# Output products of a unit one gap later, column-norm loads one step ahead, whole-row sums in the last pair

## The chip, the cores and the metric

The kernel runs on one core of one Trainium2 chip. The metric is the device time of one execution in microseconds (us), the median of several runs; lower is better. Engines are named as in the profile: PE is TensorE (PEld its weight loads), ACT is ScalarE, DVE is VectorE, POOL is GpSimd, SP is SyncE. POOL and SP issue the transfers (DMAs) that this text speaks of.

## The reference

Channel attention, then a feed-forward layer with SiLU and no gate of its own:

```python
qn = q / (norm(q, axis=1) + 1e-06); kn = k / (norm(k, axis=1) + 1e-06)   # q, k, v: 2 x 6016 x 256
s  = kn.transpose(0, 2, 1) @ qn / tau                                   # 2 x 256 x 256
a  = softmax(s)
x  = (v @ a).reshape(12032, 256)
h  = x @ w_in                                                           # 256 -> 2048
out = (h / (1 + exp(-h))) @ w_out                                       # 2048 -> 256
```

## The kernel before, in words

The output is made in twelve pairs (`pairs`): for each of the two batches b, five of 1024 tokens and one of 896. The attention matrix is folded into `w_in` (`mix`), so a pair needs two large products, v times the mixed weights and the SiLU of that times `w_out`. Each f32 operand is split into a high and a low f16 part and three products of the parts are made; both products use a seven-product (Strassen-Winograd) scheme, so sums and differences of blocks are operands too.

Pairs 0 and 5 go through `emit_pair_group`. The other ten (`paired`) go through `emit_unit`: eight units u each, U0 to U7 below, four of which (`q` from 0 to 3) add into one set of four PSUM banks, named a, b, c and d. A unit has four gaps; each begins with input products (`product`, six matmuls each: three in gap 0, two in gap 1, one each in gaps 2 and 3), and then the main loop pops output products from the list `ready`, up to a cost of 8, 12, 16 and 8, where each entry costs 4 and is four matmuls: 2, 3, 4 and 2 entries, 11 in all. The input products go through the three banks y, x and z, which ACT copies and DVE subtracts (`minus`), then ACT applies SiLU (`silu`), rounds the result to the high f16 part (`high`), and DVE makes the low part (`rest`). The upper two blocks of a unit are b11 and b12 (`tops`), the lower two b21 and b22 (`lows`).

`out_of_unit` queues what follows a unit. Its output products are lists: `now` (seven entries, from b11 to b22 themselves), `then` (from the sums t1, t2, t3) and one from t4 that goes behind the next unit's. The sums and the products are not emitted at once. `later(n, ...)` hangs a call on the n-th gap from here, and `tail` runs what hangs on the current gap. t1 (= b11 + b12) and, but for the last unit of four, t4 (= t2 + b21) are made by pairs of DMAs on POOL's queue, a copy and then one that adds (`accum_op`) and therefore waits for the copy to land; t2 and t3 are DVE's (`plus`). At the fourth unit of each set, ACT takes the four banks out (`take`), DVE joins them (`join`), and `leave` adds and stores.

In the ten paired pairs the order of instructions on PE, DVE and ACT is the order of the program text (`manual_schedule`), and each engine works through its own list strictly in that order. POOL and SP also execute their own lists in order.

Beside the units run steps of other work, spread by the main loop behind the gaps: `scale_v` (the next pair's v: maximum, scale, splits; three steps a unit), the loads of the next v, and, in pairs 1 to 3, `square_sums`: 24 steps, one a unit in gap 1, that each load a stretch of the transposed q or k of the second batch (tile `turned`) and have ACT sum its squares. `turned` and the tile of t2 and t3 (`t23`) rotate through the same seven buffers (`st`).

Of the kernel before, what the change touches and what calls it, by code (L numbers as in the profile page):

```python
# [9 lines left out]
F32 = mybir.dt.float32  # L10
# [4 lines left out]
AF = mybir.ActivationFunctionType  # L15
ALU = mybir.AluOpType
AX = mybir.AxisListType
PSUM = bass.MemoryType.PSUM
P = 128
# [11 lines left out]
def channel_attention_then_silu_ffn(ctx, tc, kq, qT, kT, vT, tau, w_in, w_out, outT):  # L31
    nc = tc.nc
    B, N, _, C = kq.shape
    DFF = w_in.shape[1]
    KC = C // P
# [4 lines left out]
    NT = 1024  # L40
# [40 lines left out]
    def room(name, n=1):  # L81

        k = turns[name] + turns[name] % n
        size = rooms[name].shape[1]
        k %= size
        turns[name] = (k + n) % size
        return rooms[name][:, k] if n == 1 else rooms[name][:, k : k + n]
# [158 lines left out]
    def square_sums():  # L246

        edges = list(range(0, N, NT)) + [N]
        m = sm.tile([P, 2 * KC, len(edges) - 1], F32, tag="squares", name="squares", bufs=1)
        norms[0] = m  # L250
        yield
        for i, x in enumerate((qT, kT)):
            for cb in range(KC):
                for g, (u, w) in enumerate(zip(edges, edges[1:])):
                    t = st.tile([P, NT], F32, tag="st", name="turned", bufs=7)
                    nc.sync.dma_start(t[:, : w - u], x[cb * P : (cb + 1) * P, u:w])
                    sq = st.tile([P, NT], F32, tag="sq", name="sq", bufs=2)
                    nc.scalar.activation(
                        out=sq[:, : w - u], in_=t[:, : w - u], func=AF.Square,
                        accum_out=m[:, i * KC + cb, g : g + 1],  # L260
                    )
                    yield

    def attention(b):

# [433 lines left out]
    def emit_unit(p, u):  # L699


        b, n, w = pairs[p]
        h = w // 2
        m, alpha, sg = parts[p]
        which = 2 * (u % 4), 2 * (u % 4) + 1
        wide = h // 2
        at = u // 4 * wide

        def product(bank, a, x, first=False):
            for k, i in enumerate(which):  # L710
                for j, (v, c) in enumerate(((1, 0), (0, 1), (0, 0))):
                    nc.tensor.matmul(  # L712
                        bank[:, k * wide : (k + 1) * wide], mixed[b, i][:, v, a - 1],
                        m[:, c, x, at : at + wide], start=(first and j + k == 0),
                        stop=(j == 2), skip_group_check=True,
                    )

        def minus(g, a, c):
            nc.vector.tensor_tensor(out=g, in0=a[:, :h], in1=c[:, :h], op=ALU.subtract)  # L719

        def silu(src, g):
            nc.scalar.activation(out=g, in_=src, func=AF.Silu, scale=alpha)  # L722

        top, low = room("g", 2)[:, :, :h], room("g", 2)[:, :, :h]
        tops, lows = room("hl", 2)[:, :, :, :h], room("hl", 2)[:, :, :, :h]

        def high(hl, g):
            nc.scalar.activation(out=hl[:, :, 0], in_=g, func=AF.Copy, scale=sg)  # L728

        def rest(hl, g):  # L730
            nc.vector.scalar_tensor_tensor(  # L731
                out=hl[:, :, 1], in0=g, scalar=sg, in1=hl[:, :, 0], op0=ALU.mult,
                op1=ALU.subtract,
            )

        product(y, S1, T1, True)
        c51 = hp.tile([P, 2, 512], F32, tag="c51", name="c51")
        nc.scalar.copy(c51[:, 0, :h], y[:, :h])  # L738
        product(x, A11, B11, True)
        nc.scalar.copy(c51[:, 1, :h], x[:, :h])  # L740
        product(z, A12, B21, True)
        tail(0)
        minus(top[:, 0], c51[:, 1], z)
        yield
        product(y, S4, B22)
        product(x, S2, T2)
        c2 = hp.tile([P, 512], F32, tag="c2", name="c2")
        nc.scalar.copy(c2[:, :h], x[:, :h])  # L748
        silu(top[:, 0], top[:, 0])
        tail(1)  # L750
        minus(top[:, 1], c2, y)
        yield
        product(x, S3, T3)
        minus(low[:, 1], x, c51[:, 0])
        silu(top[:, 1], top[:, 1])
        tail(2)
        yield
        product(x, A22, T4)
        silu(low[:, 1], low[:, 1])
        silu(x[:, :h], low[:, 0])  # L760
        high(tops, top)
        tail(3)
        out_of_unit(
            p, u, [tops[:, 0], tops[:, 1], lows[:, 0], lows[:, 1]], lambda: rest(tops, top),
            lambda: high(lows, low), lambda: rest(lows, low),
        )
        yield
# [4 lines left out]
    def tail(slot):  # L772

        for run in tails.pop(ticks[0], ()):
            run()
        ticks[0] += 1

    def later(slot, *those):
        tails.setdefault(ticks[0] + slot, []).extend(those)
# [3 lines left out]
    sums = {}  # L783
# [3 lines left out]
    def out_of_unit(p, u, blocks, rest_top, high_low, rest_low):  # L787
# [4 lines left out]
        t, q = divmod(u, 4)  # L792
        end = q == 3
        last = end and t and p == len(pairs) - 1
        b11, b12, b21, b22 = blocks
        if "14" not in sums:
            sums["14"] = vp.tile([P, 2, 2, 2, 512], F16, tag="v", name="sums", bufs=3)
        t23 = st.tile([P, 2, 2, 512], F16, tag="st", name="t23", bufs=7)
        t1, t4 = (sums["14"][:, u % 2, k, :, :h] for k in range(2))
        t2, t3 = (t23[:, k, :, :h] for k in range(2))  # L800

        def bank(name):
            if (p, t, name) not in banks:
# [9 lines left out]
        def add(name, side, terms, last):  # L813
            def run():
                first = (p, t, name) not in banks
                o = bank(name)
                these = [
                    (weight(kind, y, 2 * q + k, e), x[:, v, k * wide : (k + 1) * wide])
                    for k in range(2) for kind, e, x, y, v in terms
                ]  # L820
                for j, (a, x) in enumerate(these):
                    nc.tensor.matmul(  # L822
                        o[:, side * wide : (side + 1) * wide], a, x,
                        start=(first and j == 0), stop=(last and j == len(these) - 1),
                        skip_group_check=True,
                    )
                if last:
                    ended.append((p, t, name, side))
            return 4, run

        def cross(kind, e, x):
            return [(kind, e, x, 1, 0), (kind, e, x, 0, 1)]

        def high(e, x1, x2):
# [10 lines left out]
        ]  # L845
        fourth = add("d", 0, cross(0, 1, t4), end)
        then = [
            add("b", 0, cross(-3, 1, t3), end),
            add("a", 1, cross(-2, 1, t2), end),
            add("b", 1, cross(-1, 1, t1), end),  # L850
            *behind_one,
        ]
# [7 lines left out]
        def take(name):  # L860
            if p not in backs:
                backs[p] = back_of(p)
            while (p, t, name, {"a": 1, "b": 1, "c": 1, "d": 0}[name]) not in ended:
                (pending or ready).pop(0)[1]()
            s[name] = hp.tile([P, 512], F32, tag="sb", name="sb", bufs=4)
            nc.scalar.activation(  # L866
                out=s[name][:, :h], in_=banks[p, t, name][:, :h], func=AF.Copy, scale=backs[p]
            )
# [14 lines left out]
        def leave(e):  # L883
            x, y = (s[k][:, :h] for k in ("ca", "db")[e])
            nc.vector.tensor_tensor(out=x, in0=x, in1=y, op=ALU.add)  # L885
            n0 = b * N + n + t * wide
            nc.sync.dma_start(
                outT[e * P : (e + 1) * P, n0 : n0 + w - t * wide]
                .rearrange("e (l n) -> e l n", l=2)[:, :, :wide] if t == 0 else
                outT[e * P : (e + 1) * P, n0 - wide : n0 - wide + w]  # L890
                .rearrange("e (l n) -> e l n", l=2)[:, :, wide:],
                x.rearrange("e (l n) -> e l n", l=2),
            )

        def plus(o, x, y):
            nc.vector.tensor_tensor(out=o, in0=x, in1=y, op=ALU.add)

        def first_sum():
            if last:
                plus(t1, b11, b12)  # L900
                return
            nc.gpsimd.dma_start(t1, b11)  # L902
            nc.gpsimd.dma_start(t1, b12, accum_op=ALU.add)  # L903

        def third_sum():
            plus(t3, b12, b22)
            ready.extend(now)

        def other_sums():
            plus(t2, t3, b11)  # L910
            if end:
                plus(t4, t2, b21)
            else:
                nc.gpsimd.dma_start(t4, t2)
                nc.gpsimd.dma_start(t4, b21, accum_op=ALU.add)  # L915
            ready.extend(then)
# [3 lines left out]
        later(2, other_sums)  # L920
        if end:
            for k, name in enumerate("cabd"):
                later(3 + k, lambda name=name: take(name))
            later(7, join, lambda: leave(0))
            later(8, lambda: leave(1))

    def prepare_sums():

# [403 lines left out]
```

## Time and profile before

| | before |
|---|---|
| time, median of 3 runs | 1136.4 us (1136.05 to 1139.99) |
| profiled execution: time, span | 1141.5 us, 1139.7 us |
| PE busy | 1034.9 us (91%) |
| DVE busy | 830.2 us (73%) |
| ACT busy | 812.4 us (71%) |
| POOL busy | 213.9 us (19%) |
| mean granted TensorE clock | 0.980 |

Busy time is that of the instructions an engine executed; what the engine waited is in the views of waits. Ends of matmuls are modelled.

### The profile page before, as it was taken

What the parts mean: (1) busy time and instruction counts of PE and PEld (TensorE: products, weight loads), DVE (VectorE), ACT (ScalarE), POOL (GpSimd) and SP (SyncE); (2) the same over time, 40 slices, a digit from 0 to 9 for tenths busy, and PEclk for the clock granted to TensorE, in tenths of its full rate; (3) what the DMA queues carried; (4) which work ended last, traced back from release to release, by engine and by line L of the source; (5) the groups of instructions that cost most, each with busy time, mean ns of one, the idle gap of its engine ahead of it and who ended that gap; (6) DMA issues with size and microseconds to landing.
All of it is one profiled execution on the core that took longest, in us unless ns stands there. A gap on an engine that the chain in (4) does not pass through costs nothing. (4 is left out here: it accounts for less than half of the span.)

```text
span 1139.7 us, 20504 instructions
## 1 busy us (share of the span) xinstructions
PE 1034.9 (91%) x8222; PEld 847.2 (74%) x8222; DVE 830.2 (73%) x1358; ACT 812.4 (71%) x1241; POOL 213.9 (19%) x301
## 2 busy tenths in 40 slices
PE   9999999989888898988999898998998998999885
PEld 8866546868777786877556787887877877888885
DVE  6997495767675776877778777777776776776654
ACT  6687687778667686776777676776776776776653
POOL 1010000212211222212000222222212222222322
PEclk9999999999998999999999999999999999999988
DMA  9993104563645636335101435436435435444533
GB/s 371 397 350 137 38 1 130 124 180 97 184 141 140 176 77 174 96 77 146 47 1 38 108 83 149 112 77 156 103 90 138 106 89 136 105 94 101 109 82 73
DMA packets 63793, 143.35 MB, mean 126 GB/s; under 512 B 6930, under 2 KB 21218, under 8 KB 63698
## 3 DMA queue, kind: packets, MB, share of 16 engines
q0 software_dynamic: 32944, 72.57, 27.5%
q1 hardware_dynamic: 30466, 68.95, 17.0%
q8 instruction: 64, 1.05, 0.4%
q10 hardware_dynamic: 288, 0.52, 0.1%
q14 instruction: 31, 0.25, 0.1%
HBM read 57.67 MB, written 12.32 MB: 61 GB/s over the span
## 5 line engine op out<-in xcount | busy, mean ns | idle before, releaser
L712 PEld LDWEIGHTS <-wall 128*128 128x128 f16 x3360 | 331.7, 99 | 52.8 <-issue 13.2
L822 PE MATMUL o<-hl,wo 128*128 128x256 f16 (+1 forms) x1920 | 254.3, 274 | 64.3 <-DVE hl L731 64.3
L822 PEld LDWEIGHTS <-wo 128*128 128x128 f16 x2240 | 222.1, 99 | 102.1 <-issue 75.0
L712 PE MATMUL x<-m,wall 128*128 128x256 f16 (+1 forms) x1920 | 263.5, 274 | 10.2 <-ACT g L722 9.9
L731 DVE SCALAR_TENSOR_TENSOR hl<-g,sg,hl 128x1024 f16<-128x1024 f32 (+1 forms) x160 | 202.7, 1267 | 87.7 <-ACT hl L728 87.0
L722 ACT ACTIVATE g<-g,alpha 128x512 f32<-128x512 f32 (+1 forms) x240 | 171.1, 717 | 92.5 <-DVE g L719 91.9
L728 ACT ACTIVATE hl<-g,sg 128x1024 f16<-128x1024 f32 (+1 forms) x160 | 182.0, 1138 | 0.0
L712 PE MATMUL y<-m,wall 128*128 128x256 f16 (+1 forms) x960 | 132.7, 275 | 0.1
L902 POOL DMA_DIRECT2D sums<-hl x79 | 49.7, 629 | 351.4 <-DVE hl L731 107.6
L903 POOL DMA_DIRECT2D sums<-hl x79 | 70.2, 889 | 221.3 <-DMA sums<-hl 158.1
L748 ACT COPY c<-x 128x512 f32<-128x512 f32 (+1 forms) x80 | 46.6, 583 | 76.3 <-PE x L712 75.0
L722 ACT ACTIVATE g<-x,alpha 128x512 f32<-128x512 f32 (+1 forms) x80 | 54.3, 679 | 51.9 <-PE x L712 51.9
L620 PE MATMUL o<-hl,wo 128*128 128x512 f16 (+1 forms) x384 | 87.2, 366 | 0.1
L915 POOL DMA_DIRECT2D sums<-hl x60 | 53.7, 896 | 174.6 <-ACT c L738 52.8
L822 PEld LDWEIGHTS <-ws_hi 128*128 128x128 f16 x640 | 63.6, 99 | 27.3 <-issue 19.9
L719 DVE TENSOR_TENSOR g<-x,c 128x512 f32<-128x512 f32 (+1 forms) x80 | 54.6, 683 | 29.8 <-PE x L712 29.8
L164 DVE SCALAR_TENSOR_TENSOR m<-v_t,sv,m 128x512 f16<-128x512 f32 (+2 forms) x46 | 34.8, 761 | 55.1 <-ACT m L163 54.9
L822 PE MATMUL o<-t,ws_hi 128*128 128x256 f16 (+1 forms) x320 | 74.5, 271 | 0.0
L822 PE MATMUL o<-t,ws_lo 128*128 128x256 f16 (+1 forms) x320 | 74.5, 271 | 0.0
L293 PE MATMUL sc<-kq_t 128*128 128x256 f32 x320 | 73.5, 381 | 0.4 <-DMA kq_t<-in_kq 0.4
L822 PEld LDWEIGHTS <-ws_lo 128*128 128x128 f16 x640 | 63.6, 99 | 7.5
L293 PEld LDWEIGHTS sc<-kq_t 128*128 128x128 f32 x320 | 60.0, 190 | 10.9 <-DMA kq_t<-in_kq 1.6
(188 smaller groups left out, 1612.0 us busy)
## 6 DMA issues: line engine op xcount, KB each, us to landing
sums<-hl POOLq DMA_DIRECT2D x198, 256.0 KB, 3.3
kq_t<-in_kq SPq DMA_DIRECT2D x39, 512.0 KB, 8.6
sums<-t POOLq DMA_DIRECT2D x54, 256.0 KB, 2.4
v_t<-in_vT SPq DMA_DIRECT2D x10, 1024.0 KB, 5.3
outT<-sb SPq DMA_DIRECT2D x40, 256.0 KB, 2.7
turned<-in_qT SPq DMA_DIRECT2D x10, 512.0 KB, 5.4
turned<-in_kT SPq DMA_DIRECT2D x10, 512.0 KB, 6.7
sums<-hl POOLq DMA_DIRECT2D x20, 224.0 KB, 3.7
```

The source lines that it names most:

```text
L293: nc.tensor.matmul(sc[:, cb, :], t[:, i, 0, cb * P : (cb + 1) * P], t[:, i, 1, :], start=(j + i == 0 and cb == 0), stop=(j + i == J - 1), ...
L620: nc.tensor.matmul(o[:, :h], a[:, f, ee], hl[:, m, :h], start=(c == 1 and i == 0), stop=(c == NF and i == 2),)
L712: nc.tensor.matmul(bank[:, k * wide : (k + 1) * wide], mixed[b, i][:, v, a - 1], m[:, c, x, at : at + wide], start=(first and j + k == 0), ...
L719: nc.vector.tensor_tensor(out=g, in0=a[:, :h], in1=c[:, :h], op=ALU.subtract)
L722: nc.scalar.activation(out=g, in_=src, func=AF.Silu, scale=alpha)
L728: nc.scalar.activation(out=hl[:, :, 0], in_=g, func=AF.Copy, scale=sg)
L731: nc.vector.scalar_tensor_tensor(out=hl[:, :, 1], in0=g, scalar=sg, in1=hl[:, :, 0], op0=ALU.mult, op1=ALU.subtract,)
L748: nc.scalar.copy(c2[:, :h], x[:, :h])
L822: nc.tensor.matmul(o[:, side * wide : (side + 1) * wide], a, x, start=(first and j == 0), stop=(last and j == len(these) - 1), skip_group_ ...
L902: nc.gpsimd.dma_start(t1, b11)
L903: nc.gpsimd.dma_start(t1, b12, accum_op=ALU.add)
L915: nc.gpsimd.dma_start(t4, b21, accum_op=ALU.add)
```

## The change

- `third_sum` no longer releases `now`; `other_sums` does, one gap later, just ahead of `then`. So the seven products of `now` are popped from gap 2 of the next unit on, and `then` from gap 0 of the one after, each one gap later than before.
- In `then`, the product of t2 (bank a) comes ahead of that of t3 (bank b).
- The bank takes hang on the fourth to seventh gap behind the unit, not the third to sixth; `join` stays on the seventh, and the two `leave` calls go from the seventh and eighth to the tenth and eleventh.
- `tail(3)` stands ahead of the last two SiLUs and the rounding of `tops`, not behind them.
- The DMAs that make t1 move whole 512-column rows of the blocks, in the pair of 896 tokens too, where the blocks use only 448 of them.
- `square_sums` issues the load of a stretch one step ahead of the squares that read it. It has one step more.

```diff
+        def load(i, cb, g):
+            u, w = edges[g : g + 2]
+            t = st.tile([P, NT], F32, tag="st", name="turned", bufs=7)
+            nc.sync.dma_start(t[:, : w - u], (qT, kT)[i][cb * P : (cb + 1) * P, u:w])
+            return t[:, : w - u], m[:, i * KC + cb, g : g + 1]
+
+        todo = [(i, cb, g) for i in range(2) for cb in range(KC) for g in range(len(edges) - 1)]
+        ahead = load(*todo.pop(0))
+        yield
+        while ahead:
+            t, sum_ = ahead
+            sq = st.tile([P, NT], F32, tag="sq", name="sq", bufs=2)
+            nc.scalar.activation(
+                out=sq[:, : t.shape[1]], in_=t, func=AF.Square, accum_out=sum_
+            )
+            ahead = load(*todo.pop(0)) if todo else None
+            yield
...
-        tops, lows = room("hl", 2)[:, :, :, :h], room("hl", 2)[:, :, :, :h]
+        whole = room("hl", 2), room("hl", 2)
+        tops, lows = (k[:, :, :, :h] for k in whole)
...
         product(x, A22, T4)
+        tail(3)
         silu(low[:, 1], low[:, 1])
         silu(x[:, :h], low[:, 0])
         high(tops, top)
-        tail(3)
...
         then = [
+            add("a", 1, cross(-2, 1, t2), end),
             add("b", 0, cross(-3, 1, t3), end),
-            add("a", 1, cross(-2, 1, t2), end),
             add("b", 1, cross(-1, 1, t1), end),
...
-            nc.gpsimd.dma_start(t1, b11)
-            nc.gpsimd.dma_start(t1, b12, accum_op=ALU.add)
+            nc.gpsimd.dma_start(w1, blocks[0])
+            nc.gpsimd.dma_start(w1, blocks[1], accum_op=ALU.add)
 
         def third_sum():
             plus(t3, b12, b22)
+
+        def other_sums():
             ready.extend(now)
-
-        def other_sums():
             plus(t2, t3, b11)
...
             for k, name in enumerate("cabd"):
-                later(3 + k, lambda name=name: take(name))
-            later(7, join, lambda: leave(0))
-            later(8, lambda: leave(1))
+                later(4 + k, lambda name=name: take(name))
+            later(7, join)
+            later(10, lambda: leave(0))
+            later(11, lambda: leave(1))
```

## Rows read from the trace of the kernel before

**Rows 1.** Who PE waited for, whole span: total us, times, longest.
```profile
PE o L822 <- DVE hl L731: 64.3, 61, 2.3
PE o L822 <- DMA sums<-hl: 17.9, 8, 4.9
PE x L712 <- ACT g L722: 9.9, 5, 3.7
```
**Rows 2.** Timeline, pair 7 into pair 8: start, duration, instruction, [idle before, releaser].
```profile
761.76 0.49 PE L822 MATMUL o<-hl,wo 128*128 128x256 f16 x3 [1.37 <-DVE hl L731]
...
772.99 0.92 PE L822 MATMUL o<-hl,wo 128*128 128x256 f16 x7 [1.80 <-DVE hl L731]
772.99 0.64 PEld L822 LDWEIGHTS <-wo 128*128 128x128 f16 x6 [1.97 <-issue]
...
845.69 0.49 PE L822 MATMUL o<-hl,wo 128*128 128x256 f16 x3 [1.37 <-DVE hl L731]
```
**Rows 3.** Timeline: the first product of two successive units, with no wait between.
```profile
788.68 0.82 PE L712 MATMUL y<-m,wall 128*128 128x256 f16 x6
...
798.07 0.82 PE L712 MATMUL y<-m,wall 128*128 128x256 f16 x6
```
**Rows 4.** Timeline of ACT and DVE from one unit's last product on.
```profile
776.15 0.82 PE L712 MATMUL x<-m,wall 128*128 128x256 f16 x6
...
778.63 0.71 ACT L163 ACTIVATE m<-x,sv 128x512 f16<-128x512 f32 x1
...
779.38 0.75 DVE L164 SCALAR_TENSOR_TENSOR m<-x,sv,m 128x512 f16<-128x512 f32 x1 [2.82 <-ACT m L163]
...
782.66 1.28 DVE L731 SCALAR_TENSOR_TENSOR hl<-g,sg,hl 128x1024 f16<-128x1024 f32 x1
...
784.58 0.68 DVE L719 TENSOR_TENSOR g<-c,y 128x512 f32<-128x512 f32 x1
```
**Rows 5.** Who ACT waited for, whole span: total us, times, longest.
```profile
ACT sq L258 <- DMA turned<-in_kT: 16.5, 3, 6.7
ACT sq L258 <- DMA turned<-in_qT: 10.0, 2, 6.8
```
**Rows 6.** Timeline around one of these waits: SP's issues, ACT, PE.
```profile
332.51 1.66 SPq L887 DMA_DIRECT2D outT<-sb  x2
...
336.69 12.13 SPq L256 DMA_DIRECT2D turned<-in_kT  x4
...
343.04 1.06 ACT L258 ACTIVATE sq<-turned 128x1024 f32<-128x1024 f32 x1 [6.74 <-DMA turned<-in_kT]
...
346.64 1.44 PE L712 MATMUL x<-m,wall 128*128 128x256 f16 x6 [3.74 <-ACT g L722]
```
**Rows 7.** Who PE waited for in the last pair, 1045 to 1140 us.
```profile
PE o L822 <- DMA sums<-hl: 12.7, 5, 4.9
```
**Rows 8.** Line 902, the first copy of t1, in the last pair.
```profile
DMA to landing us min/median/max: 2.5/3.8/5.6
```
**Rows 9.** Line 902 in the pairs before it, 620 to 1040 us.
```profile
DMA to landing us min/median/max: 2.3/2.7/4.4
```
**Rows 10.** POOL's timeline: the copies of t1 in the last pair, then in pair 7.
```profile
1074.59 1.20 POOL L902 DMA_DIRECT2D sums<-hl  x1
1078.68 1.20 POOL L903 DMA_DIRECT2D sums<-hl  x1 [2.89 <-DMA sums<-hl]
...
1084.49 1.23 POOL L902 DMA_DIRECT2D sums<-hl  x1
...
771.08 0.56 POOL L902 DMA_DIRECT2D sums<-hl  x1 [2.61 <-ACT c L748]
773.71 0.86 POOL L903 DMA_DIRECT2D sums<-hl  x1 [2.07 <-DMA sums<-hl]
```
**Rows 11.** Windows by stage: us, busy us (instructions) of PE, PEld, DVE, ACT, POOL, granted clock, DMA share, GB/s.
```profile
200.00:550.00 350.00, 308.50 (x2643) 263.50 (x2641) 249.44 (x401) 255.81 (x393) 77.38 (x109) 0.97 0.50 133
...
1050.00:1140.00 90.00, 70.90 (x676) 67.27 (x673) 50.47 (x77) 49.91 (x79) 25.58 (x27) 0.91 0.41 86
```

More of the change, by code (lines that the diff above doesn't have):

```diff
@@ L251, in square_sums @@
         yield
[L252 to L262, printed above, removed]
+        def load(i, cb, g):
[14 more added lines that the diff above has]
+            yield
     def attention(b):
@@ L761, in emit_unit @@
         high(tops, top)
-        tail(3)
         out_of_unit(
-            p, u, [tops[:, 0], tops[:, 1], lows[:, 0], lows[:, 1]], lambda: rest(tops, top),
+            p, u, [k[:, i] for k in whole for i in range(2)], lambda: rest(tops, top),
             lambda: high(lows, low), lambda: rest(lows, low),
@@ L794, in out_of_unit @@
         last = end and t and p == len(pairs) - 1
-        b11, b12, b21, b22 = blocks
+        b11, b12, b21, b22 = (k[:, :, :h] for k in blocks)
         if "14" not in sums:
@@ L798, in out_of_unit @@
         t23 = st.tile([P, 2, 2, 512], F16, tag="st", name="t23", bufs=7)
-        t1, t4 = (sums["14"][:, u % 2, k, :, :h] for k in range(2))
-        t2, t3 = (t23[:, k, :, :h] for k in range(2))
+        w1, w4 = (sums["14"][:, u % 2, k] for k in range(2))
+        t1, t4, t2, t3 = (k[:, :, :h] for k in (w1, w4, t23[:, 0], t23[:, 1]))
         def bank(name):
```

## The prediction

> **What bounds the kernel now.** I read the busy shares first, then the waits of PE, then the timeline of single units, because a mean over the span hides where a wait ends. PE is the busiest engine, and it never waits for its own banks or weights; it waits for operands. The view of its waits has three lines that matter [rows 1]: 64.3 us in 61 pieces for the low parts that DVE makes (`rest`), 17.9 us for the sums that POOL's DMAs make, 9.9 us for SiLU on ACT. In the timeline the first kind recurs with every pair: the mark at 761.76 comes again at 845.69, so a pair takes 83.93 us [rows 2]. A unit in which PE waits for nothing runs from 788.68 to 798.07, 9.39 us [rows 3], eight of them 75.1 us. The 8.8 us between the two are waits. They stand in gap 1, at the second entry of `now`, which needs b21's low part: at 772.99 PE's last matmul had ended 1.80 us before, while the weight loads had stood for 1.97 us [rows 2]. So each wait costs some 0.17 us more than its line says, as the array drains. 61 x 0.17 is 10.4, and the first kind costs 74.7 us in all.
>
> **The change, part by part.**
>
> *Products one gap later.* Nothing is added on PE: eleven entries a unit, in the same numbers per gap. But the entry that waited now stands in gap 2, behind the rest of gap 1 (12 matmuls) and the products of gap 2 (6): 18 matmuls more. 86 matmuls make the unit of 9.39 us, so one takes 0.109 us, and the entry comes 1.96 us later against the same DVE. Nearly every recorded wait of this kind is shorter than that (the longest is 2.3, rows 1). The products of t2, t3 and t1 move by one gap too, so their operands gain time as well; none of them is late next.
>
> What is late next is a chain, and it bounds this term. With PE no longer stopping in gap 1, DVE and ACT get no pause to catch up. From the start of a unit's last product (776.15) it goes over SiLU and rounding to the split of v that `scale_v` puts behind them on ACT (778.63), its low part on DVE (779.38), the two `rest` with a subtraction and another split between (782.66), t3, and then two subtractions from 784.58 [rows 4]. A subtraction of 0.68 starts some 0.61 before the next can, so the second ends at 784.58 + 0.61 + 0.68 = 785.9, and the next unit's last product, which overwrites the bank that it reads, can start then: 785.9 - 776.15 is 9.8 us, 0.4 above the 9.39 that PE needs. That holds in units where a split stands in gap 3, four a pair by the order of the steps of `scale_v`, in nine pairs (the last prepares none): 36 x 0.45 us is 16 us that stay. This term gives 74.7 - 16 = 58.7 us. Its bounds are 74.7, if no chain shows, and about 26, if every one of the 80 units takes 10.0 us (80 x 0.6 = 49 stay).
>
> `tail(3)` ahead of the SiLUs and the later takes add no instruction. A take (0.7 us on ACT) now stands ahead of two SiLUs in two units a pair; it needs products that PE has run in the gap before, so I cost it at nothing, and if PE were late there it would cost its lateness 20 times. The two `leave` leave the stretch in which `join` and the next unit's `rest` compete for DVE; that is in the 36 units above.
>
> *Loads a step ahead.* ACT stands 26.5 us, in five pieces, for a stretch of transposed q or k [rows 5]. In the timeline SP comes to these loads late: it stands in front of the two stores until 332.51, issues the load at 336.69, ACT gets it at 343.04 after 6.74 us of idleness, and PE stops for 3.74 us [rows 6]. With the load in the program text one unit (some 10 us) ahead of its use, and the stores three gaps later than before, the load has no store ahead of it that it waited for in this case. PE's side of these stops is the 9.9 us for SiLU and, just behind two of them and in pair 1, 5.2 of the 17.9 us for sums (17.9 less the last pair's 12.7, rows 1, 7), with eight drains (1.4) 16.5 us. The added step costs one square of 1.06 us [rows 6] on ACT at the head of pair 4; I take 0.5. Net 16. The bounds are 0, if SP's order leaves the loads behind the stores, and 16.
>
> *Whole rows in the last pair.* PE waits 12.7 us there for sums [rows 7]. The copy and the adding DMA of a unit follow each other on POOL with two landings between, then the two DMAs of t4: the cycle is 1084.49 - 1074.59 = 9.9 us [rows 10], while PE needs 86 matmuls of 224 columns, 9.39 x 224/256 = 8.2. POOL's queue is the bound of this stage. An issue over two runs of 448 columns takes 1.20 us and the next waits 2.89 behind it; over one run of 512 columns it takes 0.56 and 2.07 [rows 10]. By the median from issue to landing a copy takes 3.8 us in the last pair and 2.7 before it [rows 8, 9]. So a copy of a whole row lands 1.1 us sooner though it moves more bytes, and the adding one gains about as much in issue: some 1.5 us of the cycle, 9.9 to 8.4. Together with the gap that t1 gains the waits nearly go; at the very end PE still has to wait for the last unit's own chain, some 3 us. The term is 12.7 + 0.9 for drains - 3, about 10 us; its bounds are 4 and 13.6. The Trainium skill (DMA: Bandwidth & Descriptors, Anatomy of one DMA — SWDGE (gpsimd) path) puts the time of such a DMA at 2.0 us plus its bytes over 436 GB/s, and in "Why small descriptors are slow (HBM only)" says that transfers inside SBUF don't pay for small pieces. By that the whole rows would cost 0.07 us each (an estimate from its figures) and gain nothing; the landings of this trace say otherwise, so I go by them.
>
> *Clock.* The granted clock is 0.97 from 200 to 550 us and 0.91 from 1050 to 1140 [rows 11]: 0.03 x 350 + 0.09 x 90 = 18.6 us lost, and it falls behind the stops: the six matmuls at 346.64 took 1.44 us where 0.82 is usual [rows 4, 6]. I take back a good half, 10 us, with 0 and 18 as bounds.
>
> Sum: 58.7 + 16 + 10 + 10 = 94.7 us. The profiled execution took 1141.5 us (span 1139.7), so it would take 1046.8. The median of the runs is 5.1 us below that execution; I take the same saving from it: 1136.4 - 94.7 = **1041.7, say 1042 us**.
>
> **The rivals.**
>
> *A: DVE and ACT become the bound.* The chain above is 9.8 us against PE's 9.39, and in pairs 1 to 3 ACT has a square a unit on top. If every unit takes 10.0 us, the first term is 26: 26 + 16 + 10 + 8 = 60, 1076 us. For it: the margin is 0.4 us. Against it: units without a wait exist [rows 3], in which the same engines kept up with PE.
>
> *B: the loads don't come sooner.* SP's order isn't fixed by hand; if the loads stay behind the stores, the 16 us and half of the clock's 10 stay: 74 saved, 1062 us. For it: SP issues four loads in a row once it is free [rows 6], so its place in the queue decides, not the step. Against it: the stores themselves move back.
>
> *C: whole rows bring nothing* and POOL stays the bound of the last pair at 9.9 us a cycle: that term shrinks to 4, 1048 us. For it: the 2.89 us lie behind a DMA of t4 that is under way too [rows 10], so the two runs a row need not be their cause. Against it: the medians of the landings. The Trainium skill's rule above would give this case.
>
> *D: slower.* The place is the end of a set of four units. The product of t1, now third in gap 1, needs two DMAs in a row; if they land late by X, PE stops there, and the take of b, t4's last product, the take of d, now ahead of two SiLUs on ACT, and `join` are all late behind it. 20 such ends must each lose more than 94.7/20 = 4.7 us before the kernel is slower. Only the longest wait for sums, 4.9 us [rows 1], is of that size, and it falls in the last pair, where POOL's cycle is longest. At 5.5 us each it would be 1152.
>
> **How the numbers follow.** The forecast has 0.58, A 0.15, B 0.12, C 0.09, D 0.06. The forecast alone lies between 1022 (nothing stays of the first term: 1136.4 - 74.7 - 16 - 13.6 - 10) and 1068 (the 0.45 us stay in all 72 units of the nine pairs, 32 us, and the last two terms come to half: 42.7 + 16 + 5 + 5). The range reaches up to A's 1076. A difference of 0.5% is about what a measurement of this kernel can tell from none. All cases but D are far more than 0.5% faster: 0.94 for faster. Of D's 0.06, 0.02 is for a D that just eats the gain and 0.04 for slower.
>
> **What would show it.** Right: the waits of PE for L731 fall from 64.3 to under 20 us; a pair of the second batch takes 77 us instead of 83.9; no line of ACT waiting for `turned`; the last pair's waits for sums under 4 us; copies of t1 there landing in about 2.7 us; the granted clock at 0.99 or more up to pair 10. Wrong: a new line of PE waiting for `minus` or for ACT's copies with more than 30 us (A); `turned` still in ACT's waits (B); PE waiting for sums in all pairs (D).

## The result and the profile after

The changed kernel takes 1070.66 us (median of 4 runs, 1069.8 to 1074.39), the kernel before 1138.2 us beside it: a ratio of 0.9411, 95% interval 0.9376 to 0.9446, or 67.5 us less. The forecast was 94.7 us less (1042 us), its range 1022 to 1076 us. The sign was right and the range held the time, but the forecast's own range ended at 1068; the rest of the range, up to 1076, belonged to rival A. 27 us of the expected gain did not come.

The profiled execution spans 1068.8 us, 70.9 less than before. The view of whom PE waited for, whole span (total us, times, longest), answers to [rows 1]; lines have moved: 731 is now 739, 719 is 726, 722 is 729, 822 is 830.

```profile
PE o L830 <- DMA sums<-hl: 17.3, 12, 4.5
PE x L719 <- DVE g L726: 13.9, 27, 1.5
PE x L719 <- ACT g L729: 6.2, 9, 0.8
PE x L719 <- ACT c L756: 1.3, 2, 0.7
PE o L830 <- DVE hl L739: 0.8, 1, 0.8
```

The reader is to see two things. The line that the change was aimed at is gone: 61 waits and 64.3 us have become one wait of 0.8. And three lines stand in its place: PE now stops in front of an input product, for DVE's subtractions (`minus`), 27 times, and for SiLU, 9 times, and the sums from POOL's DMAs are waited for 12 times where it was 8, for nearly the same total.

Where these stand is seen in PE's timeline over one pair of the second batch (start, duration, instruction, idle before and its releaser), which answers to [rows 2]:

```profile
654.40 0.82 PE L719 MATMUL x<-m,wall 128*128 128x256 f16 x6 [0.56 <-DVE g L726]
...
721.71 0.81 PE L719 MATMUL x<-m,wall 128*128 128x256 f16 x6 [0.31 <-DVE g L726]
724.81 0.82 PE L719 MATMUL x<-m,wall 128*128 128x256 f16 x6 [0.76 <-ACT g L729]
732.76 0.81 PE L719 MATMUL x<-m,wall 128*128 128x256 f16 x6 [0.56 <-DVE g L726]
742.88 0.81 PE L719 MATMUL x<-m,wall 128*128 128x256 f16 x6 [0.56 <-DVE g L726]
```

From the mark at 654.40 to that at 732.76 a pair takes 78.36 us; it was 83.93. All stops lie within three successive units. Between the first products of units (703.83, 713.37, 723.23, 734.28 and 744.41) the unit ahead of these three takes 9.54 us, and they take 9.86, 11.05 and 10.13. Of the other four units of a pair, three take the 9.39 us of one without a wait [rows 3]. From 732.76 to 742.88, from one stop to the next, it is 10.12 us.

The same unit on ACT and DVE answers to [rows 4]:

```profile
731.43 0.68 DVE L726 TENSOR_TENSOR g<-c,y 128x512 f32<-128x512 f32 x1
...
732.14 0.72 ACT L729 ACTIVATE g<-g,alpha 128x512 f32<-128x512 f32 x1 [2.40 <-DVE g L726]
...
733.99 0.67 ACT L729 ACTIVATE g<-x,alpha 128x512 f32<-128x512 f32 x1
734.56 1.14 ACT L736 ACTIVATE hl<-g,sg 128x1024 f16<-128x1024 f32 x1
735.60 0.71 ACT L163 ACTIVATE m<-x,sv 128x512 f16<-128x512 f32 x1
736.35 0.75 DVE L164 SCALAR_TENSOR_TENSOR m<-x,sv,m 128x512 f16<-128x512 f32 x1 [1.18 <-ACT m L163]
737.01 1.28 DVE L739 SCALAR_TENSOR_TENSOR hl<-g,sg,hl 128x1024 f16<-128x1024 f32 x1
...
739.63 1.28 DVE L739 SCALAR_TENSOR_TENSOR hl<-g,sg,hl 128x1024 f16<-128x1024 f32 x1
...
741.55 0.68 DVE L726 TENSOR_TENSOR g<-c,y 128x512 f32<-128x512 f32 x1
742.15 0.68 DVE L726 TENSOR_TENSOR g<-x,c 128x512 f32<-128x512 f32 x1
```

It is the chain that the prediction named: rounding on ACT, the split of v behind it (735.60), its low part on DVE, which has idled 1.18 us for it with `rest` queued behind (736.35), the two `rest`, and at 742.15 the subtraction that PE waits for at 742.88. But it does not start at PE's product, as the prediction had it. The SiLU that reads this product (733.99) has no idle time before it. ACT runs without a pause from 732.14, where it had waited 2.40 us for the subtraction of 731.43, and that subtraction comes again at 741.55, 10.12 us later. The loop closes on ACT and DVE alone, and PE follows it.

SP and ACT: no line of ACT waits for `turned` any more. The granted clock is 0.996 in the mean. By stage (us, busy us of PE, PEld, DVE, ACT, POOL, clock, DMA share, GB/s; [rows 11] before):

```profile
200.00:500.00 300.00, 280.79 (x2523) 246.42 (x2522) 233.97 (x379) 243.49 (x374) 73.76 (x104) 1.00 0.57 151
1050.00:1069.00 19.00, 8.64 (x60) 7.15 (x57) 7.35 (x12) 3.44 (x5) 2.81 (x3) 0.78 0.28 63
```

In pairs 1 to 3 the clock is full; only the end is still slow. POOL's timeline in the last pair ([rows 10] before; line 910 is the copy of t1, 911 the DMA that adds, 922 and 923 the two of t4):

```profile
990.14 0.55 POOL L910 DMA_DIRECT2D sums<-hl  x1 [2.83 <-PE z L719]
992.67 0.85 POOL L911 DMA_DIRECT2D sums<-hl  x1 [1.98 <-DMA sums<-hl]
...
999.18 1.21 POOL L923 DMA_DIRECT2D sums<-hl  x1 [3.36 <-ACT hl L736]
999.93 1.05 POOL L910 DMA_DIRECT2D sums<-hl  x1
1003.93 0.87 POOL L911 DMA_DIRECT2D sums<-hl  x1 [2.95 <-DMA sums<-hl]
...
1009.00 1.21 POOL L923 DMA_DIRECT2D sums<-hl  x1 [3.47 <-DVE t L904]
```

The copy of a whole row lands 1.98 us after its issue has ended when it stands alone (990.14), and 2.95 when it stands right behind t4's adding DMA (999.93). From 999.18 to 1009.00 the cycle is 9.8 us, where it was 9.9. So this cycle has hardly changed, and from 985 us on PE waits 7.6 us for the sums in three pieces, the longest 4.5.

### The profile page after: what moved, and what is told of

Its sections match the earlier page's. It is cut to its first block, busy times and chain, and to the rows that moved or that the text cites. A ratio compares the mean times of both kernels' runs of the same rounds, so it can differ in the third digit from the quotient of the medians.

```text
span 1068.8 us, 20527 instructions
## 1 busy us (share of the span) xinstructions
PE 1017.0 (95%) x8222; PEld 839.8 (79%) x8222; DVE 826.9 (77%) x1358; ACT 811.4 (76%) x1241; POOL 210.5 (20%) x301
## 3 DMA queue, kind: packets, MB, share of 16 engines
q8 instruction: 64, 1.05, 0.4%
## 4 chain that ended last, share of the span: by engine, by line
PE 50%; DVE 16%; ACT 14%; issue 10%; DMA 7%; POOL 2%; POOLq 0%; DVEq 0%; ACTq 0%
PE o L830 18%; PE x L719 10%; PE o L627 5%; PE sc L300 5%; PE y L719 4%; DVE hl L739 4%; ACT hl L736 4%; DVE g L726 4%; DMA sums<-t 3%; DMA sums<-hl 3%; ACT g L729 3%; ACT m L163 2%; PE x L658 2%; PE z L719 2%; DVE t L904 2%
## 5 line engine op out<-in xcount | busy, mean ns | idle before, releaser
L719 PEld LDWEIGHTS <-wall 128*128 128x128 f16 x3360 | 327.5, 98 | 67.6 <-issue 32.4
L719 PE MATMUL x<-m,wall 128*128 128x256 f16 (+1 forms) x1920 | 259.1, 271 | 22.0 <-DVE g L726 13.9
L830 PE MATMUL o<-hl,wo 128*128 128x256 f16 (+1 forms) x1920 | 248.5, 273 | 0.8 <-DVE hl L739 0.8
L830 PEld LDWEIGHTS <-wo 128*128 128x128 f16 x2240 | 220.0, 98 | 25.9 <-issue 1.1
L719 PE MATMUL y<-m,wall 128*128 128x256 f16 (+1 forms) x960 | 129.6, 271 | 0.1
L911 POOL DMA_DIRECT2D sums<-hl x79 | 67.9, 859 | 248.8 <-DMA sums<-hl 191.9
L910 POOL DMA_DIRECT2D sums<-hl x79 | 55.0, 697 | 264.1 <-DVE hl L739 99.4
L923 POOL DMA_DIRECT2D sums<-hl x60 | 53.8, 896 | 198.2 <-ACT hl L736 30.2
L756 ACT COPY c<-x 128x512 f32<-128x512 f32 (+1 forms) x80 | 46.3, 579 | 54.8 <-PE x L719 53.9
L830 PE MATMUL o<-t,ws_lo 128*128 128x256 f16 (+1 forms) x320 | 76.7, 271 | 0.0
L830 PE MATMUL o<-t,ws_hi 128*128 128x256 f16 (+1 forms) x320 | 76.7, 271 | 0.0
L726 DVE TENSOR_TENSOR g<-x,c 128x512 f32<-128x512 f32 (+1 forms) x80 | 54.4, 680 | 21.9 <-PE x L719 21.9
L627 PEld LDWEIGHTS <-wo 128*128 128x128 f16 x384 | 37.6, 98 | 39.0 <-issue 0.8
```

The lines of the kernel that those rows point to most:

```text
L627: nc.tensor.matmul(o[:, :h], a[:, f, ee], hl[:, m, :h], start=(c == 1 and i == 0), stop=(c == NF and i == 2),)
L719: nc.tensor.matmul(bank[:, k * wide : (k + 1) * wide], mixed[b, i][:, v, a - 1], m[:, c, x, at : at + wide], start=(first and j + k == 0), ...
L830: nc.tensor.matmul(o[:, side * wide : (side + 1) * wide], a, x, start=(first and j == 0), stop=(last and j == len(these) - 1), skip_group_ ...
L910: nc.gpsimd.dma_start(w1, blocks[0])
L911: nc.gpsimd.dma_start(w1, blocks[1], accum_op=ALU.add)
```

## The experiments

Ten kernels ran, each beside the kernel before on the same chip; ratios are to it. Its medians there were 1137.1 to 1138.4 us, so times are also set against the changed kernel's 1070.66 us. The order of t2 and t3 in `then` and the later takes were not run by themselves.

**The change in its parts.** `gap_only` has the later products, takes, leaves and the moved `tail(3)`, with the old `square_sums` and these DMAs:

```diff
-            nc.gpsimd.dma_start(w1, blocks[0])
-            nc.gpsimd.dma_start(w1, blocks[1], accum_op=ALU.add)
+            nc.gpsimd.dma_start(t1, b11)
+            nc.gpsimd.dma_start(t1, b12, accum_op=ALU.add)
```

> The products one gap later with the takes, the leaves and tail(3) as in the changed kernel, but the loads of transposed q and k in their old place and the last pair's DMAs over 448 columns. Theory (the gap carries nearly all): 53 to 60 us faster than before, 1078 to 1085 us, because the stops for the transposed loads cost about 10 us with their clock and stay. Rival (the loads matter more than that, about 20 us or more): 1088 us or above. Either way the waits of PE for L731's low parts are nearly gone.

1087.64 us, ratio 0.9566 (0.9539 to 0.9594): 50.6 us faster. Between the two expectations, and nearer to the rival: the gap carries three quarters of the gain, and the rest of the change 17 us. PE waits for SiLU 21.9 us here, behind the ACT that still stands 23.6 us for `turned`; the granted clock is 0.987. For the sums it waits 2.0 us in pairs 1 to 3 and 11.8 us in the last pair.

`load_only` is the kernel before with the new `square_sums` alone.

> Only the loads of transposed q and k one step ahead. Theory (as predicted, 16 us for waits and some of the clock): 10 to 20 us faster than before, 1118 to 1128 us, and no line of ACT waiting for the tile turned. Rival (SP's order decides, not the step): ACT still waits for it in the units behind the stores, within 3 us of before.

1133.21 us, ratio 0.995 (0.992 to 0.998): 5.1 us faster, below the theory's 10 and above the rival's 3. ACT's waits for `turned` are gone, as the theory has it. What went wrong with the gain is in PE's waits:

```profile
PE o L828 <- DMA sums<-hl: 28.9, 19, 5.3
```

PE no longer waits for SiLU (9.9 us before) but for the sums: 28.9 us in 19 pieces, where it was 17.9 in 8. What ACT no longer holds up is held up by POOL's DMAs. The same view for pairs 1 to 3 alone (185 to 530 us), in the kernel before, here, in `gap_only` and in the changed kernel:

```profile
PE o L822 <- DMA sums<-hl: 5.3, 3, 2.4
...
PE o L828 <- DMA sums<-hl: 16.1, 13, 3.4
...
PE o L823 <- DMA sums<-hl: 2.0, 2, 1.0
...
PE o L830 <- DMA sums<-hl: 9.7, 9, 1.9
```

With or without the later products, the loads a step ahead add 8 to 11 us of these waits, and the later products take 3 to 6 of them away. Loads ahead are worth 5.1 us alone; loads and whole rows together are worth 17.0 once the products stand a gap later (1087.64 - 1070.66), the granted clock rising from 0.987 to 0.996 with them.

`rows_only` is the kernel before with only the DMAs of t1 over whole rows.

> Only the DMAs of t1 over whole rows. Theory of the prediction: the copy lands in 2.7 us and POOL's cycle in the last pair falls from 9.9 to about 8.4 us, 5 to 10 us faster than before. Rival (from the trace of the changed kernel, where copies of whole rows landed in 3.7 us by the median and the cycle stayed at 9.8): the copy stands behind the adding DMA of t4, not behind its own pieces, and the time is within 3 us of before.

1137.56 us against 1138.27, ratio 0.9996 (0.9974 to 1.0017): by the time, the rival. The copies behind t4's adding DMA still have 2.95 us to their landing; the cycle is 9.4 us here, from 1066.45 to 1075.86, where it was 9.9:

```profile
1066.45 1.21 POOL L916 DMA_DIRECT2D sums<-hl  x1 [2.89 <-ACT c L741]
1067.21 1.05 POOL L903 DMA_DIRECT2D sums<-hl  x1
1071.21 0.87 POOL L904 DMA_DIRECT2D sums<-hl  x1 [2.95 <-DMA sums<-hl]
...
1075.86 1.21 POOL L916 DMA_DIRECT2D sums<-hl  x1 [3.04 <-DMA sums<-t]
```

Yet the rows do something in the last pair. PE's waits for sums there, here (from 1045 us) and in `gap_only` (from 985 us), which has the old rows:

```profile
PE o L823 <- DMA sums<-hl: 9.4, 5, 4.3
...
PE o L823 <- DMA sums<-hl: 11.8, 4, 5.4
```

They were 12.7 us before [rows 7] and are 7.6 in the changed kernel. So whole rows took 3.3 us of waits away alone and 4.2 in the combination, in one execution each. Alone it does not show in the time: in the same execution PE waits 67.6 us for low parts, where it was 64.3 [rows 1].

**The chain.** `split_moved` is the changed kernel with two steps of `scale_v` behind gap 2 and none behind gap 3.

```diff
-  slot in ((0, 2, 3) if p in paired else ...
+  slot in ((0, 2) if p in paired or not last else ...
-  vgen = background(vgen, 2 if p == 0 else 1)
+  vgen = background(vgen, 2 if p == 0 or (p in paired and slot == 2) else 1)
```

> The changed kernel with the step of scale_v that stood behind gap 3 put behind gap 2, where two steps now stand. Theory (a chain of ACT and DVE through that split sets the pace of four units a pair): the waits of PE for the subtractions and SiLU in the paired pairs, 13.9 and 6.2 us, fall to less than a third, and 12 to 22 us go, 1049 to 1059 us. Rival (DVE is full in those units, whatever the order): the waits stay or move, within 4 us of the changed kernel's 1070.7.

1056.91 us, ratio 0.9293 (0.9264 to 0.9321): 13.8 us faster than the changed kernel, with the same instructions on every engine. The subtractions have left PE's waits:

```profile
PE x L719 <- ACT g L729: 7.6, 10, 1.3
...
PE x L719 <- ACT c L756: 1.3, 2, 0.7
PE x L719 <- DVE g L726: 1.3, 3, 0.6
```

13.9 us in 27 pieces have become 1.3 in 3. DVE was not full; it stood for ACT in the wrong place. The theory had SiLU's 6.2 us fall too; they are 7.6, so the split's place in gap 3 is not what these come from (`tail_back`, below).

**The sums.** `loads_left_out` loads one transposed stretch instead of 24 and squares it each time.

```diff
-            t = st.tile([P, NT], F32, tag="st", name="turned", bufs=7)
-            nc.sync.dma_start(t[:, : w - u], (qT, kT)[i][cb * P : (cb + 1) * P, u:w])
+            if not kept:
+                kept.append(st.tile([P, NT], F32, tag="st", name="turned", bufs=7))
+                nc.sync.dma_start(kept[0], qT[:P, :NT])
+            t = kept[0]
```

> The changed kernel with one load of a transposed stretch instead of 24; ACT squares that one stretch 24 times, so the column norms of the second batch are left out. Theory (SP's loads, several in a row behind the stores, slow the landing of POOL's DMAs in pairs 1 to 3): PE's nine waits for sums there, 9.7 us, nearly vanish, 6 to 14 us faster than the changed kernel, 1057 to 1065 us. Rival (POOL's own queue of four DMAs a unit is too slow for the faster units): the waits stay above 7 us and the time within 4 us of 1070.7.

1061.95 us, ratio 0.9341 (0.9308 to 0.9375): 8.7 us faster than the changed kernel. In the changed kernel PE waits in pairs 1 to 3 for (185 to 500 us):

```profile
PE o L830 <- DMA sums<-hl: 9.7, 9, 1.9
PE x L719 <- DVE g L726: 6.5, 11, 1.5
PE x L719 <- ACT g L729: 2.5, 4, 0.8
```

and without the loads, in the same stretch:

```profile
PE x L723 <- DVE g L730: 7.7, 14, 1.5
PE x L723 <- ACT g L733: 2.5, 4, 0.8
```

The line of the sums is gone, so the waits for them there come from the loads, and not from the length of POOL's own queue. The longest landing of t1's copy falls from 7.1 to 5.5 us, its median from 3.5 to 3.3, and POOL's own waits for these copies from 85.8 to 58.5 us. That the loads come in rows, three or four behind SP's stores, is what the timeline shows; spreading them was not tried.

`t1_on_dve` adds t1 on DVE in all units of the last pair.

```diff
-            if last:
+            if last or p == len(pairs) - 1:
                 plus(t1, b11, b12)
                 return
```

> The changed kernel with t1 of all units of the last pair added on DVE, so that POOL has only t4's two DMAs a unit there. Theory (POOL's cycle of 9.8 us sets the pace of the last pair): the three waits for sums there, 7.6 us, and the low clock behind the longest of them go, 6 to 12 us faster, 1059 to 1065 us. Rival (DVE's eight added instructions of 0.62 us take the place, or the end is bound by the last unit's own chain): within 3 us of 1070.7.

1061.74 us, ratio 0.934 (0.9305 to 0.9376): 8.9 us faster than the changed kernel, as the theory has it. In the last pair (985 us on) this line alone is left of PE's waits, and the granted clock is 0.999 in the mean of the whole span, where it was 0.996:

```profile
PE o L830 <- DVE hl L739: 1.2, 1, 1.2
```

**The smaller edits.** `old_leaves` puts the calls of `leave` back:

```diff
-            later(7, join)
-            later(10, lambda: leave(0))
-            later(11, lambda: leave(1))
+            later(7, join, lambda: leave(0))
+            later(8, lambda: leave(1))
```

> The changed kernel with the two calls of leave back on the seventh and eighth gap behind the unit. Theory (DVE has little room there, and SP's stores then stand ahead of the loads again): 4 to 12 us slower than the changed kernel, with new waits of PE for subtractions. Rival (the leaves' place doesn't matter once the products have moved): within 3 us.

1075.57 us, ratio 0.9459 (0.9415 to 0.9503). 4.9 us slower, but its interval and that of the changed kernel overlap. The waits lean to the theory: PE waits for low parts 10 times, 4.9 us, where it was once, 0.8 us. They are not the subtractions that it named.

`tail_back` puts `tail(3)` behind the SiLUs and the rounding again.

> The changed kernel with tail(3) behind the SiLUs and the rounding again, so that the take of bank d and join come after them in gap 3. Theory (as predicted, its place costs nothing either way): within 3 us of 1070.7. Rival (the take ahead of the SiLUs delays the chain of gap 3, and 20 takes of 0.6 us are to be had): 4 to 12 us faster. Rival (d's bank is needed in gap 3 and a late take stops PE): 4 us slower or more.

1071.48 us, ratio 0.9421 (0.9378 to 0.9464): no difference. Yet the waits differ, PE's whole span:

```profile
PE x L719 <- DVE g L726: 14.6, 28, 1.5
PE y L719 <- ACT c L746: 2.8, 8, 0.4
...
PE x L719 <- ACT g L729: 1.5, 8, 0.2
```

SiLU's line falls from 6.2 to 1.5 us and one for ACT's copy of y (2.8 us in 8 pieces) appears. In the changed kernel ACT comes to that SiLU as follows; PE's stop of 0.76 us at 724.81 stands behind it:

```profile
721.71 0.67 ACT L874 ACTIVATE sb<-o,back 128x512 f32<-128x512 f32 x1
722.28 0.71 ACT L163 ACTIVATE m<-v_t,sv 128x512 f16<-128x512 f32 x1
722.90 0.67 ACT L874 ACTIVATE sb<-o,back 128x512 f32<-128x512 f32 x1
723.47 0.71 ACT L729 ACTIVATE g<-g,alpha 128x512 f32<-128x512 f32 x1
724.08 0.68 ACT L729 ACTIVATE g<-x,alpha 128x512 f32<-128x512 f32 x1
```

Two takes (L874) and a split stand ahead of the two SiLUs, and the second take is the one that `tail(3)` put there: the edit costs at that place what it gives a gap later. At the other end of a set in the pair (760.83 to 762.58) the takes come without a split, and PE does not stop. So it is takes and split together; how the 0.76 us divide between them is not shown.

**A faster version.** `split_and_t1` is `split_moved` and `t1_on_dve` together.

> The split's step moved and the last pair's t1 on DVE, together. Theory (two separate stages, so the gains add): 1056.9 less 6 to 12, 1045 to 1051 us. Rival (DVE is fuller with both): no better than 1054.

1048.16 us, ratio 0.922 (0.9181 to 0.926): 22.5 us faster than the changed kernel, where the two alone gave 13.8 and 8.9. The gains add.

`split_t1_last` moves the product of t1 behind that of t4 besides:

```diff
-            add("b", 1, cross(-1, 1, t1), end),
             *behind_one,
+            add("b", 1, cross(-1, 1, t1), end),
```

> As split_and_t1, but the product of t1 stands behind the one of the t4 before it, four matmuls (0.44 us) later. Theory (PE is early for t1 in pairs 1 to 3 by up to 3.1 us, and t4 has long landed): the eight waits for sums, 8.8 us, shrink by 0.44 us each, 3 to 4 us in all, 1044 to 1046 us. Rival (t4 is as late as t1): within 1 us of 1048.2.

1046.58 us (1044.03 to 1050.14), ratio 0.9196 (0.9156 to 0.9237). The waits for sums fall from 8.8 to 6.8 us, some half of what the theory had; the times of the two versions can't be told apart. It is the fastest median here.

## Why the prediction was right, and where it was 27 us off

Terms below go by the profiled executions, with 0.17 us for each wait as in the prediction; their sum, some 74 us, is within 4 of the 70.9 by which the span fell. The gap brought 45.8 us instead of 58.7, the loads some 5 instead of 16, the whole rows and the gap in the last pair 5.4 instead of 10, the clock 18 instead of 10. So three terms were too large and one too small, and that the time lay within the range was in part luck: it was held by the bound of rival A, which did not happen. Three of the signs of being right failed: a pair takes 78.4 us, not 77; PE still waits 7.6 us for sums in the last pair, not under 4; t1's copies land there in 3.7 us by the median, not 2.7.

*The gap.* Right that the waits for low parts go, and right about what comes instead: a chain through the split in gap 3 that delays four units a pair (9.54, 9.86, 11.05 and 10.13 us). The step had the chain start at PE's product and SiLU start as soon as that has ended, 9.8 us; the loop is 10.12, because ACT is held by the late subtraction and comes to that SiLU later: from the product to the split it is 735.60 - 732.76 = 2.84 us, where [rows 4] have 2.48. This cost little. The 27 stops for subtractions make 13.9 + 27 x 0.17 = 18.5 us, where 16 were left for the chain, and `split_moved` showed that they are this chain: 24 of the 27 went with it. The mis-sized term is another, the takes, which the prediction put at nothing. The 9 stops for SiLU, behind the takes of the end of a set and a split, are 6.2 + 9 x 0.17 = 7.7 us, and they stay when the split leaves gap 3. The 2 stops for ACT's copies are 1.6 and the low part that is left 1.0. So 28.8 us stayed instead of 16, and the term gave 45.8 instead of 58.7 us.

*The loads.* The step "with the loads ahead PE's waits for SiLU and for sums in pairs 1 to 3 go, 16 us" failed in its second half. ACT's waits went, and so did SiLU's 10.8 us. The waits for sums there, taken as a consequence of ACT's stops, come from the loads themselves (`loads_left_out`), and issuing the loads a step ahead made them longer: 16.1 us instead of 5.3 with the loads alone, 9.7 instead of 2.0 behind the gap. It is not the faster units, for `gap_only` has them too and waits 2.0. Why loads that come sooner get more in the way of POOL's DMAs is not shown; in the view of SP's waits they now wait 54.8 us for t4's copies, where it was 19.5 (t4's source t2 lies in the buffers that `turned` shares). By waits the term is about 5 us. Rival B, loads that come no sooner, was wrong: ACT never waits for them.

*Whole rows.* The step "a copy of a whole row lands 1.1 us sooner" was wrong, and rival C was right about why. The medians that it compared, 3.8 and 2.7 us [rows 8, 9], come from copies in different places: in the last pair most stand behind t4's adding DMA. Compared in the same place the two runs a row cost the landing next to nothing. Alone, the copy over 448 columns in the kernel before needed 2.05 us behind its issue:

```profile
1054.32 0.73 POOL L902 DMA_DIRECT2D sums<-hl  x1 [4.16 <-PE o L822]
1057.10 1.22 POOL L903 DMA_DIRECT2D sums<-hl  x1 [2.05 <-DMA sums<-hl]
```

against 1.98 for a whole row (992.67), and behind t4's DMA 2.89 [rows 10] against 2.95. The rule of the Trainium skill (DMA: Bandwidth & Descriptors, "Why small descriptors are slow (HBM only)"), that transfers inside SBUF don't pay for small pieces, agrees with these four numbers, and was set aside for medians that mixed two cases. What the rows do shorten is the issue: behind t4's DMA 1.05 us instead of 1.20 for the copy, and 0.87 instead of 1.20 for the adding DMA. Four cycles of POOL in the last pair (from one of t4's adding DMAs to the next, two in each half of the pair) took 41.7 us before and 39.5 with the rows alone, 44.3 with the gap alone and 41.7 in the changed kernel: some 0.6 us a cycle less, where 1.5 were foreseen. Of the 10 us, 5.1 + 2 x 0.17 = 5.4 came in the combination, by the waits some 4 of them from the rows (11.8 us in `gap_only`, 7.6 here) and 1 from the gap. So C was near in its price of 4 us and wrong that the rows bring nothing.

*The clock.* Mis-sized the other way: counted as in the prediction, 0.020 of 1139.7 us were lost before and 0.004 of 1068.8 are now, so 18 us came back where 10 were taken, an estimate from the mean clock. With PE's stops in pairs 1 to 3 no longer than 1.9 us, where the longest was 3.7 [rows 1], the granted clock is 1.00 between 200 and 500 us; it was 0.97 from 200 to 550 [rows 11].

*Rival A* named the right engines. It had every unit at 10.0 us; two of eight take 10.1 or more, three 9.39, and the pair 78.36 / 8 = 9.8 a unit. *Rival D*: no end of a set costs anything like 4.7 us, but the take ahead of the SiLUs, where a split stands beside it, does stop PE for 0.76 us a time, and gives as much back elsewhere (`tail_back`).

Still open: whether the later `leave` calls are worth 4.9 us, why the loads a step ahead delay the sums more than late ones did, and how much of the waits for sums would stay if SP's loads were spread.

## What to carry to other kernels

When a wait is moved out of a pipelined loop, the engines that had caught up during it lose their pause: follow the chain through every engine's queue, the background work in it too, and move that work out of the chain together with the wait. A transfer that is issued early can still delay others (here PE's waits for POOL's sums rose with it), so look at whose landing it lengthens. Compare landings only between DMAs that stand in the same place of their queue.

## What the runs showed of the hardware that was not expected

- A SBUF copy of 256 KB on POOL's queue lands 1.98 us after its issue ends when alone and 2.95 us when right behind an adding DMA; cutting each row in two (224 KB then) moves neither by more than 0.07 us. It shows in the issue: 0.73 us instead of 0.55 for the copy alone, 1.21 instead of 0.87 for the adding one.
- Loads of 512 KB on SP's queue, several in a row, go with copies of 256 KB on POOL's queue that take up to 7.1 us to land, where 2.3 is the least; with the loads left out the longest is 5.5.
- Moving one ACT and DVE pair of 0.7 us each by one gap, four times a pair, was worth 13.8 us over the kernel, although DVE was busy 77% of the span and ACT 76%.
